# 71 groups instead of 74 take SIGN, 16 products left out, and new orders on all five engines

## Chip, core and metric

The kernel runs on one core of one Trainium2 chip. The metric is the device time of one execution in microseconds (us). A core has five engines with a queue each: PE (TensorE, matmul; PEld is its weight load), DVE (VectorE), ACT (ScalarE), POOL (GpSimd) and SP (SyncE, which here only issues DMAs). Each runs its own list of instructions strictly in the order in which they were written and waits on semaphores for the others.

## What is computed

Attention that keeps, for each query, the 32 largest scores, then a two-layer net with squared ReLU on the joined heads. Cut to what matters:

```python
# q, k, v: (8, 8, 576, 64)
scores = q @ k.T / sqrt(64)
kth = 32nd largest of each row
attn = softmax(where(scores >= kth, scores, -1e9))
x = (attn @ v) as (4608, 512)
h = x @ w_in            # 512 x 2048
out = (max(h, 0) ** 2) @ w_out
```

## The kernel before

**Groups.** The queries are cut into 144 groups, each 128 queries of two heads (the last 64 queries of two pairs of heads share a group). For each group, in this order: PE multiplies q and k (`mm`, L875) into a PSUM area of three banks; ACT copies the 2 x 576 scores out (L1053); DVE folds them with three maxima of PSUM and SBUF (L1131); POOL makes the matching minima with two integer operations (L1126); DVE finds the 8 largest of several candidate lists (MAX8, L1178, L1173), strikes them out (MATCH_REPLACE8, preceded by a MATCH_VALUE_LOAD, both L1193) and ends with the 32nd largest (`kth`, L1196); ACT makes a mask from it (L1219, two instructions); PE transposes the scores and adds the mask (L878, L875); ACT takes the exponential (L1285); PE multiplies with v. A second PSUM area of the same kind holds the transposed scores.

**SIGN groups.** Of the three strikings of a group (`c8`, `c16`, `c24`), the last can be done in another way: for the groups in `VOID`, DVE issues no MATCH_REPLACE8 for `c24`; ACT computes SIGN of the difference to the 24th value, with an accumulated sum (L1183: two ACTIVATEs, each with a read of the accumulator), and POOL multiplies (L1186). `VOIDS` holds the ranges of these groups, and the sums go to `signs`.

**The net.** Every 256 or 128 finished rows are transposed by DMA into `xt`, PE multiplies with `win`, ACT applies ReLU (L1443), POOL or ACT squares (L1458, L1461), PE multiplies with `wo`, ACT copies out (L1479), and SP stores. The last rows go another way (`feed_last`: ReLU at L1527, squares on DVE at L1530).

**The verdict.** The fast way to find the 32nd value can fail on rare inputs. `verdict` gathers checks on DVE (L1703 to L1729), PE sums them (L1731), and DVE writes `flag` (L1733). Each engine loads `flag` at the end (L1778), and branches to a full second computation if it isn't 0. So nothing ends before `flag`. Three checks per range in `VOIDS` are tensor operations (L1703): `x` compares the 23rd and 24th values, `y` subtracts from `signs`, `z` compares the 22nd and 24th values.

**What sets the order.** The program first makes a list of operations, then `arrange` puts them on the engines by the table `ORDER`: one row of operation numbers per engine. A negative number in PE's row is an idle product (three 128x128 products with `ident_bf`, which leave nothing behind); the operations of `fill` are products of `ones_bf` with itself, 512 columns, whose result isn't used either. `SLOT` gives each PSUM tile its area. The waits follow from the order.

Of the kernel before, what the change touches and what calls it, by code (L numbers as in the profile page):

```python
# [32 lines left out]
        "90 91 92 93 94 95 96 97 98 2541 2542 2543 2547 2574 2579 101 100 104 106 102 2613 2614 2615 2620 2648 -4979 -4979 -4979 -4979 -4979 126 119 129 134 "  # L33
        "2686 136 2688 135 2687 -5025 2577 2693 148 149 2756 153 159 2758 2757 2605 2721 167 169 2607 2646 183 2763 188 3230 190 -4991 195 -4991 -4991 3232 "
        "3231 2675 2792 204 210 207 209 2677 2719 2874 -5037 219 -5037 -5037 222 -5037 -5037 226 -5037 -5037 240 -5037 -5037 2904 2748 244 241 -5049 2933 2750 "
        "-5149 2790 245 3298 2963 2819 256 257 274 3299 2992 3300 275 276 278 2900 3026 2821 2931 283 293 292 3369 3057 2959 294 3371 -5408 3370 -5408 -5408 "
        "-5169 3085 2961 2902 2990 2826 2827 2829 2830 3116 3018 2833 3437 2834 -5195 -5195 -5195 3144 3438 -5249 3053 3236 3020 -5215 3439 -5215 3083 2836 "
        "2837 3055 3264 2840 2841 3112 3304 -5244 -5244 -5244 2847 2848 2843 2844 3142 2850 3332 3114 2851 3171 2854 2857 3375 3173 2856 2861 2860 2864 2855 "
        "2866 3262 3403 2859 2858 2865 3291 2869 3942 2870 3443 3330 2871 3293 2868 2867 3471 3179 3180 3182 3183 3359 3186 3187 3189 3190 3553 3401 3193 3194 "
        "3361 3584 3196 3197 3943 3430 3200 3201 3613 3944 3432 3469 3203 4010 3204 3643 -5459 4011 4012 -5459 3672 3207 3498 3210 4081 3208 3214 -5471 3706 "  # L40
        "3500 3212 3580 3209 3211 3213 4082 3611 3737 4083 3582 -5535 3765 3217 4149 3222 3639 3218 3223 3224 3220 3221 3219 3670 3796 3505 3506 3508 3509 "
        "3824 3512 3513 3515 3516 3641 3698 3519 3520 3522 3523 3948 3733 3526 4150 3527 3976 4151 3529 3530 3700 3763 4016 3533 3538 3735 3534 3792 3539 4044 "
        "3822 3535 3536 3540 3537 3794 3851 4087 3543 3544 3853 3548 4115 3549 3546 3974 4622 3547 3550 3545 4003 4624 4623 4155 4042 4005 3859 3860 4183 3862 "
        "3863 3866 3867 4071 3869 3870 4265 4113 3873 3874 4073 -5809 4295 3876 4142 3877 3880 3881 4324 4144 4690 3907 3909 3910 3908 4181 4692 4691 4355 "
        "3918 3919 3912 3914 3913 3915 4210 3920 3921 3923 3924 3925 3926 4384 3883 4212 3884 4418 4761 4762 4291 3887 4763 3892 3889 3891 3893 3894 4449 3890 "
        "3888 4293 4322 3897 3902 3900 3899 3904 4351 4477 4829 4382 3903 4353 3898 3901 4508 3929 3932 4830 3931 3930 4410 3933 4536 4412 3934 3935 3936 4831 "
        "4445 4628 4217 4218 4447 4475 4220 4221 4656 4504 4224 4225 4227 4228 4696 4506 4534 4231 4232 4234 4235 4724 4238 4239 4241 4242 4245 4248 4247 4246 "
        "4563 4767 4251 4252 4565 4795 4255 4250 4262 4249 4261 4256 4257 5334 4260 4654 4258 4259 4835 4683 4571 4572 4574 4575 4722 4863 4578 -6143 -6143 "
        "4945 4579 4581 4582 4751 4685 4585 4586 4975 4588 4589 4793 4592 4593 4595 4596 5004 4822 4753 5335 5336 5402 5034 4824 5403 5404 4861 5063 5473 4890 "
        "4599 5474 4606 4600 5098 4892 4971 4603 4604 5475 4601 4605 4602 4973 5129 5002 4609 4612 4611 4616 5157 5541 4610 5030 4615 4897 4898 5188 4613 4614 "  # L50
        "5032 5061 4900 4901 4904 4905 5216 4907 4908 5090 4911 4912 4914 5340 5125 5092 4915 -6361 5368 5127 5155 5542 4918 4919 -6377 5543 5408 4921 4922 "
        "4925 4928 5184 4929 5436 5214 4927 4930 5186 4931 4926 5243 5479 4932 5245 5366 4935 4937 4936 4938 5507 4940 4939 4942 6014 4941 5395 5547 6015 5397 "
        "5434 5251 5252 5254 5255 5575 5258 5259 5261 5262 5657 5265 5266 5268 5269 5463 5272 5299 5273 5300 5301 5302 5687 5304 5310 5305 5307 5306 5313 5312 "
        "5311 5505 5315 5317 5318 5465 5316 5716 5534 6023 5275 5276 5746 5536 6016 5573 5279 6024 5281 5284 5282 5280 6025 5283 5775 5602 5289 5285 5295 5286 "
        "5292 5809 5604 5290 5296 5291 5293 6062 5294 5840 6063 6064 5683 5321 5326 5325 5685 5714 5869 5323 5328 6071 5742 5327 6072 5900 5773 5322 5324 5744 "
        "6073 -6920 -6920 5928 5801 5609 5610 5612 5613 6029 5803 5836 5616 5617 5619 5620 6077 5867 5623 5624 5838 -6771 -6771 6144 5626 5627 5630 5631 5633 "
# [607 lines left out]
def bass_top_k_attn__then__act_relu_squared_kernel(  # L664
# [91 lines left out]
    VOIDS = (3, 137, 2), (6, 137, 20)  # L756
# [1087 lines left out]
```

## Time and profile before

| | |
|---|---|
| median of 3 runs | 744.73 us (744.64 to 747.37) |
| the profiled execution | 746.16 us, of which the span of its instructions is 744.3 us and 1.9 us lie around it |
| busy | PE 706.4, DVE 719.4, ACT 717.3, POOL 685.9 us |

The span runs from the first to the last instruction. An engine's busy time is the union of its instructions' records. Records of DVE and ACT overlap, since the next one starts before the one ahead has ended; what an instruction costs its engine is read from start to start. A short wait can lie hidden below such an overlap.

### The profile page before, as it was taken

How to read it: one execution, taken by the hardware profiler on the slowest of the kernel's cores; microseconds unless marked ns; L12 is line 12 of the kernel's file. 1: busy time of each engine (PE TensorE's matmuls, PEld its weight loads, DVE VectorE, ACT ScalarE, POOL GpSimd, SP SyncE). 2: the span in 40 equal slices, each digit the busy share in tenths (PEclk: the TensorE clock that was granted, in tenths of full speed). 3: DMA queues.
4: the chain of work that ended last, by engine and by line, in shares of the span. 5: the costliest groups of instructions: out<-in, count | busy, mean ns of one | idle time of the engine just before them, and what ended most of it. 6: DMA issues, size and time to landing. Idle time of an engine off the chain costs nothing.

```text
span 744.3 us, 27788 instructions
## 1 busy us (share of the span) xinstructions
PE 706.4 (95%) x10712; PEld 530.0 (71%) x10712; DVE 719.4 (97%) x3397; ACT 717.3 (96%) x1276; POOL 685.9 (92%) x529
## 2 busy tenths in 40 slices
PE   8898899999999999989999999999999999999997
PEld 4565777767677676767778677777777777777876
DVE  5999999999999999999999999999999999999996
ACT  4899999999999999999999999999999999999984
POOL 3799999999999999999999999999999999999971
PEclk9999999999999999999999999999999999999999
DMA  9766544254342432134311733121643115211101
GB/s 181 165 170 175 134 102 73 70 87 78 67 84 48 84 79 52 44 70 85 82 35 36 125 92 64 27 48 56 117 75 80 28 44 93 58 35 32 37 16 51
DMA packets 172730, 57.31 MB, mean 77 GB/s; under 512 B 157744, under 2 KB 164912, under 8 KB 172592
## 3 DMA queue, kind: packets, MB, share of 16 engines
q1 hardware_dynamic: 164528, 51.19, 30.2%
q0 software_dynamic: 7392, 4.13, 4.7%
q8 instruction: 85, 1.39, 0.8%
q14 instruction: 53, 0.43, 0.2%
q10 hardware_dynamic: 672, 0.16, 0.1%
HBM read 40.83 MB, written 13.57 MB: 73 GB/s over the span
## 4 chain that ended last, share of the span: by engine, by line
ACT 59%; PE 21%; DVE 16%; issue 3%; ACTq 0%
PE ps L875 17%; ACT w L1219 16%; ACT p L1285 12%; ACT s L1053 12%; ACT g L1443 6%; ACT s L1183 5%; DVE s L1131 4%; PE ps L878 4%; DVE s L1193 3%; DVE c L1178 3%; ACT av L1388 2%; DVE kth L1196 2%; DVE s L1173 2%; ACT o L1479 2%; ACT g L1461 1%
## 5 line engine op out<-in xcount | busy, mean ns | idle before, releaser
L1126 POOL TENSOR_TENSOR u<-s 128x864 int32<-128x864 int32 x142 | 244.7, 1723 | 22.1 <-DVE s L1131 20.8
L1219 ACT ACTIVATE w<-s,kth 128x576 bf16<-128x576 f32 x286 | 245.9, 918 | 2.9 <-DVE kth L1196 2.8
L1126 POOL TENSOR_TENSOR s<-s,u 128x864 int32<-128x864 int32 x142 | 243.1, 1714 | 3.2
L1178 DVE MAX8 c<-s 128x8 f32<-128x106 f32 (+2 forms) x864 | 203.3, 264 | 0.0
L1131 DVE TENSOR_TENSOR s<-ps,s 128x288 f32<-128x288 f32 x432 | 192.2, 445 | 9.9 <-ACT s L1053 7.7
L875 PE MATMUL ps<-qk 64*128 64x192 f32 (+3 forms) x1280 | 179.5, 430 | 8.5 <-DVE s L1131 4.6
L1053 ACT COPY s<-ps 128x1152 f32<-128x1152 f32 (+1 forms) x145 | 180.2, 1244 | 4.8 <-PE ps L875 4.1
L1285 ACT ACTIVATE p<-ps 128x1152 bf16<-128x1152 f32 x143 | 180.9, 1265 | 1.7 <-PE ps L875 1.5
L1193 DVE MATCH_REPLACE8 s<-c,s 128x92 f32<-128x92 f32 (+2 forms) x716 | 179.5, 254 | 0.0
L875 PEld LDWEIGHTS ps<-qk 64*128 64x128 f32 (+1 forms) x1280 | 130.8, 176 | 39.3 <-DVE s L1131 11.4
L875 PE MATMUL ps<-wo,g 128*128 128x512 bf16 (+1 forms) x592 | 144.5, 374 | 0.8 <-ACT qk L1007 0.4
L875 PE MATMUL ps<-xt,win 128*128 128x256 bf16 (+1 forms) x1280 | 130.7, 252 | 1.7 <-ACT g L1443 0.9
L1196 DVE MAX8 kth<-s 128x8 f32<-128x296 f32 x288 | 127.9, 454 | 0.3 <-POOL s L1186 0.2
L1173 DVE MAX8 s<-s 128x8 f32<-128x288 f32 x288 | 125.3, 446 | 0.3 <-POOL s L1126 0.2
L878 PEld LDWEIGHTS ps<-ident,s 64*128 64x128 f32 x2592 | 97.0, 139 | 35.9 <-ACT w L1219 13.5
L878 PE MATMUL ps<-ident,s 64*128 64x64 f32 x2592 | 112.4, 228 | 8.8 <-ACT w L1219 7.1
L875 PEld LDWEIGHTS ps<-xt,win 128*128 128x128 bf16 x1280 | 99.0, 98 | 21.0 <-issue 4.0
L1443 ACT ACTIVATE g<-ps 128x512 bf16<-128x512 f32 x140 | 98.2, 745 | 0.2
L1458 POOL TENSOR_TENSOR g<-g 128x1024 bf16<-128x1024 bf16 x50 | 94.6, 1892 | 3.8 <-ACT g L1443 3.7
L875 PEld LDWEIGHTS ps<-wo,g 128*128 128x128 bf16 x592 | 50.2, 98 | 48.1 <-issue 4.3
L1183 ACT ACTIVATE s<-s,c 128x140 f32<-128x140 f32 x148 | 76.4, 558 | 0.0
L875 PEld LDWEIGHTS ps<-vb,p 128*128 128x128 bf16 (+1 forms) x1600 | 54.6, 101 | 22.7 <-ACT p L1285 4.5
(92 smaller groups left out, 779.0 us busy)
## 6 DMA issues: line engine op xcount, KB each, us to landing
out_dram<-o SPq DMA_DIRECT2D x32, 256.0 KB, 2.8
rk<-in_k_dram SPq DMA_DIRECT2D x63, 128.0 KB, 2.6
rq<-in_q_dram SPq DMA_DIRECT2D x62, 128.0 KB, 2.6
s<-s SPq DMA_DIRECT2D x144, 32.0 KB, 1.9
g<-in_moe_w_in_dram SPq DMA_DIRECT2D x8, 512.0 KB, 4.4
g<-in_moe_w_out_dram SPq DMA_DIRECT2D x8, 512.0 KB, 4.1
vd<-in_v_dram POOLq DMA_DIRECT2D x14, 288.0 KB, 4.5
vb<-vd SPq DMA_DIRECT2D x56, 64.0 KB, 2.3
```

Source lines behind the costliest of these rows:

```text
L875: return pe.matmul(o, l, r, start=start, stop=stop, skip_group_check=True)
L878: return pe.matmul(o, i, ident, is_transpose=True, skip_group_check=True, **kw)
L1053: return pl.op("act", .14 + 2 * (c1 - c0) / 1200, pl.at("copy", tg - LEAD + 1), lambda: act.copy(at(st)[:, :, c0:c1], two(banks(ss)[:, FIR ...
L1126: return pl.op("gp", dur, prio, lambda: gp.tensor_tensor(o().bitcast(I32), x().bitcast(I32), y().bitcast(I32), op), **kw)
L1131: return dve(.36, lambda: vec.tensor_tensor(o(), two(banks(ss)[:, FIRST_AT + c:], SECOND, QUART), x(), ALU.max), r=[ss], **kw)
L1173: prev[i] = [dve(.0685 + HALF / 960, lambda i=i: vec.max(area(LIST, LIST + 8, i), area(LESS, LESS + HALF, i)), after=prev[i] + [low], hold ...
L1178: lambda i=i, t=t, span_=span_: vec.max(eighth(t, i), span_(i)),
L1193: lambda i=i, t=t, span_=span_: vec.match_replace(span_(i), eighth(t, i), span_(i), NEG), hold=[st])]
L1196: ks.append(chain(kth, i, prev[i], .0685 + (8 + HALF) / 960, lambda i=i: vec.max(eighth(kth, i), area(BIGS - QUART, LIST + 8, i)), hold=[st]))
L1219: masks[i:] = [pl.op("act", .77, pl.at("mask", tw + .8 * i), lambda i=i: act.activation(at(wt)[:, i, :], at(st)[:, i, 0:S], ACTF.Relu, bia ...
L1285: return act.activation(at(pt)[:, :, :].rearrange("p c (h q) -> p h c q", h=2), bass.AP(x.tensor, x.offset, [x.ap[0], [APART, 2], [64, 9], ...
L1443: return act.activation(at(g)[:, g0:g0 + 512], bank(hh)[:, 0:512], ACTF.Relu)
```

## The change

- The second range of `VOIDS` has a step of 40 instead of 20: groups 26, 66 and 106 no longer take SIGN, which leaves 71 of 74. The checks on this range work on 4 groups instead of 7.
- Of PE's row, 5 of 56 `fill` products and 11 of 46 idle products are left out.
- All five rows of `ORDER` and all of `SLOT` are new. The table is one line shorter, so every line below it has a number lower by one (L1131 is L1130).

```diff
 ORDER = {
     "pe": (
...
-        "8240 8244 8246 8284"),
...
+        "8216 8231 8228 8234 8238 8236 8235 8237 8239 8242 8243 8240 8241 8281"),
...
@@ -753,7 +752,7 @@
     rzall = sb("rzall", [P, NALL])
-    VOIDS = (3, 137, 2), (6, 137, 20)
+    VOIDS = (3, 137, 2), (6, 137, 40)
     VLAST = max(v for _, v, _ in VOIDS)
```

PE's queue from its start, before and in the change (`rq` and `rk` are the first loaded pieces of q and k, `qk` their transposes; the `ones_bf` products are `fill`):

```order
L875 MATMUL ps<-ones_bf 128x512 x9
L878 MATMUL ps<-ident,rq 128x128
L878 MATMUL ps<-ident,rk 128x128 x4
L878 MATMUL ps<-ident,rk 128x64
L875 MATMUL ps<-qk 128x192
```

```order
L874 MATMUL ps<-ones_bf 128x512 x7
L877 MATMUL ps<-ident,rq 128x128
L877 MATMUL ps<-ident,rk 128x128 x4
L877 MATMUL ps<-ident,rk 128x64
L874 MATMUL ps<-qk 128x192
```

Two of the nine products ahead of the first transposes stand further back. The five `fill` products that are left out are late ones, at groups 116 to 142, and the 11 idle ones come from the middle of the row.

ACT's queue some 15 instructions after its start, before and in the change (`s` are the scores of a group, `w` its mask, `p` its exponentials, `win` a weight that is cast, `qk` the next pair's transposes):

```order
L1053 COPY s<-ps 128x2x576 x2
L1665 CAST win<-g 128x1024
L1006 COPY qk<-ps 128x512
L1008 COPY qk<-ps 128x2x64
L1219 ACTIVATE w<-s,kth 128x576 x2
L1007 COPY qk<-ps 128x512
L1285 ACTIVATE p<-ps 128x2x9x64
L1053 COPY s<-ps 128x2x576
```

```order
L1052 COPY s<-ps 128x2x576 x2
L1005 COPY qk<-ps 128x512
L1006 COPY qk<-ps 128x512
L1218 ACTIVATE w<-s,kth 128x576
L1007 COPY qk<-ps 128x2x64
L1664 CAST win<-g 128x1024
L1218 ACTIVATE w<-s,kth 128x576
L1052 COPY s<-ps 128x2x576
L1664 CAST win<-g 128x1024
L1284 ACTIVATE p<-ps 128x2x9x64
```

The copy of group 4's scores stood behind the first exponential and now stands ahead of it, and the cast of the first weight moved behind the copies of `qk` and the first mask.

DVE's queue around `x` of the verdict: before, it stood some 40 rows ahead of the last `kth`:

```order
L1196 MAX kth<-s 128x8
L1193 MATCH_REPLACE s<-c,s 128x92
L1178 MAX c<-s 128x8
L1703 TENSOR_TENSOR c<-c 128x2x67
L1193 MATCH_REPLACE s<-c,s 128x106
```

In the change it stands right behind the last `kth` of the last group (before, `y` stood there):

```order
L1177 MAX c<-s 128x8
L1192 MATCH_REPLACE s<-c,s 128x2x70
L1195 MAX kth<-s 128x8
L1702 TENSOR_TENSOR c<-c 128x2x67
L1211 TENSOR_SCALAR w<-s,kth 128x512
L1394 RECIPROCAL rzall<-av 128x4
```

And `y` has moved behind operations that wait for PE, ahead of the first L1530 (now L1529):

```order
L1374 COPY xt<-ps 128x128
L1712 TENSOR_REDUCE fone<-kth 128x1
L1724 TENSOR_REDUCE fone<-rzall 128x1
L1702 TENSOR_TENSOR signs<-signs,c 128x2x67
L1724 TENSOR_REDUCE fone<-rzall 128x1
L1529 TENSOR_TENSOR g<-g 128x256
```

Behind the last of the five L1530 stood 15 instructions of DVE up to the sum on PE; in the change 23 of them follow it, the small checks of the second range among them.

## Rows read from the trace of the kernel before

**Rows 1.** Busy time of each engine in four of five stretches of the span, in us: the stretch and its length, then PE, PEld, DVE, ACT and POOL, each with its number of instructions, the granted TensorE clock (1.00 is full speed), the share of DMA and GB/s.

```profile
0.00:20.00 20.00, 16.50 (x93) 9.31 (x93) 11.26 (x45) 9.57 (x15) 6.93 (x38) 1.00 0.90 178
20.00:80.00 60.00, 51.90 (x767) 37.74 (x769) 58.55 (x279) 55.98 (x95) 54.81 (x45) 0.94 0.68 163
80.00:700.00 620.00, 598.33 (x9196) 451.49 (x9194) 612.77 (x2909) 619.80 (x1115) 600.33 (x431) 1.00 0.33 68
...
720.00:744.30 24.30, 20.16 (x320) 16.28 (x318) 17.26 (x76) 14.33 (x28) 5.43 (x5) 0.98 0.12 39
```

**Rows 2.** Who waited for whom: of DVE in 80 to 700 us, and then of ACT and of DVE in 20 to 80 us (total, times, longest, in us).

```profile
DVE s L1131 <- ACT s L1053: 4.1, 18, 0.4
...
ACT p L1285 <- PE ps L875: 1.5, 2, 1.0
ACT s L1053 <- PE ps L875: 1.2, 2, 1.0
ACT w L1219 <- DVE kth L1196: 1.0, 1, 1.0
...
DVE s L1131 <- ACT s L1053: 1.3, 2, 0.8
```

**Rows 3.** ACT in order of time at one SIGN group: start, length, instruction. The two instructions left out repeat the first two.

```profile
34.02 0.44 ACT L1183 ACTIVATE s<-s,c 128x140 f32<-128x140 f32 x1
34.33 0.23 ACT L1183 ACTIVATION_READ_ACCUMULATOR s<-s,c 128x1 f32 x1
...
34.81 0.40 ACT L1388 COPY av<-ps 128x260 f32<-128x260 f32 x1
```

**Rows 4.** DVE in order of time at one striking of `c24` (the 140 columns), up to the start of the next instruction; and the group of POOL's multiplications on the page.

```profile
23.95 0.07 DVE L1193 MATCH_VALUE_LOAD s<-c,s 128x8 f32 x1
24.01 0.29 DVE L1193 MATCH_REPLACE8 s<-c,s 128x140 f32<-128x140 f32 x1
24.21 0.29 DVE L1178 MAX8 c<-s 128x8 f32<-128x140 f32 x1
...
L1186 POOL TENSOR_TENSOR s<-s 128x280 f32<-128x280 f32 x74 | 50.5, 683 | 10.2 <-ACT s L1183 9.6
```

**Rows 5.** The two large L1703 and their neighbours on DVE, the second stretch of the same list, and POOL's squares at those times.

```profile
712.59 1.69 DVE L1703 TENSOR_TENSOR c<-c 128x134 f32<-128x134 f32 x1
714.19 0.08 DVE L1193 MATCH_VALUE_LOAD s<-c,s 128x8 f32 x1
...
725.75 0.47 DVE L1196 MAX8 kth<-s 128x8 f32<-128x296 f32 x1
726.14 1.39 DVE L1703 TENSOR_TENSOR signs<-signs,c 128x134 f32<-128x134 f32 x1
727.45 0.47 DVE L1212 TENSOR_SCALAR w<-s,kth 128x512 bf16<-128x512 f32 x1
...
728.74 0.49 DVE L1703 TENSOR_TENSOR c<-c 128x14 f32<-128x14 f32 x2
...
712.11 1.90 POOL L1458 TENSOR_TENSOR g<-g 128x1024 bf16<-128x1024 bf16 x1
...
725.38 1.89 POOL L1458 TENSOR_TENSOR g<-g 128x1024 bf16<-128x1024 bf16 x1 [2.76 <-ACT g L1443]
```

**Rows 6.** The end on DVE, in order of time from the last square, and the chain that ended last where it passes the first L1703.

```profile
737.62 0.43 DVE L1530 TENSOR_TENSOR g<-g 128x512 bf16<-128x512 bf16 x1 [0.65 <-ACT g L1527]
...
738.33 0.37 DVE L1718 TENSOR_TENSOR c<-s,kth 128x42 f32<-128x42 f32 x2
...
740.57 0.16 DVE L1729 TENSOR_SCALAR fone<-fone 128x2 f32<-128x2 f32 x1
741.02 0.16 DVE L1733 TENSOR_REDUCE flag<-ps 1x1 int32<-1x12 f32 x1 [0.29 <-PE ps L1731]
...
712.67 1.60 DVE c L1703
```

**Rows 7.** The first products of PE in order of time; ACT's two loads of `rk`; and the loads' time from issue to landing (the last number).

```profile
1.07 4.02 PE L875 MATMUL ps<-ones_bf 128*128 128x512 bf16 x9 [1.07 <-DVE ones_bf L1622]
5.15 0.47 PE L878 MATMUL ps<-ident,rq 128*128 128x128 f32 x1
7.25 1.24 PE L875 MATMUL ps<-qk 64*128 64x192 f32 x8 [0.67 <-DVE qk L934]
...
0.76 1.25 ACTq L904 DMA_DIRECT2D rk<-in_k_dram  x2
...
rk<-in_k_dram ACTq DMA_DIRECT2D x1, 32.0 KB, 3.5
```

**Rows 8.** Busy time by stretch again, around the two stretches in which the granted clock fell; and PE's score product in the first of them.

```profile
24.00:26.00 2.00, 2.00 (x14) 1.59 (x8) 2.00 (x13) 1.13 (x1) 2.00 (x2) 0.50 1.03 292
26.00:28.00 2.00, 1.88 (x10) 0.67 (x8) 1.19 (x5) 1.75 (x3) 1.80 (x3) 0.85 0.70 61
66.00:68.00 2.00, 0.80 (x10) 0.73 (x14) 2.00 (x12) 2.00 (x4) 2.00 (x3) 0.89 0.67 151
68.00:70.00 2.00, 2.00 (x28) 1.26 (x23) 2.00 (x12) 1.76 (x2) 2.00 (x2) 0.50 0.52 85
70.00:72.00 2.00, 2.00 (x45) 1.53 (x42) 2.00 (x10) 1.39 (x5) 2.00 (x2) 0.75 0.80 277
...
23.93 2.27 PE L875 MATMUL ps<-qk 64*128 64x192 f32 x8
```

More of the change, by code (lines that the diff above doesn't have):

```diff
@@ L32 @@
     "pe": (
[43 rows of a table removed]
[L76 removed]
[38 rows of a table removed]
[L115 removed]
[121 rows of a table removed]
[42 rows of a table added]
+    "act": (
[38 rows of a table added]
+    "dve": (
[121 rows of a table added]
 }
 SLOT = (
[L239 to L240 removed]
+    "01010101010101010000100101000001010000000000001000000000100001110000000000010000000000100000000010000000000000000001000000100000000100001000"
+    "00000000000001000000000000000000100000000000000000000000000001100000001000000000010000000000000000000000000000000000000000000000000000000000"
     "00000000000000000000000000000000000000000000000000000000000000000000000000000000000000000000000000000000000000000000000000000000000000000000"
@@ L267 @@
-    "110016121001100010100111110001200111110011010030100100400010010512000006010100000101110000000011110100001201010010130012020001213011")
+    "00000000000000000000000000000000000000000000000000000000000000000000000000000000000010001000101011001100010101102000213000010011102002040101"
+    "15001000001130131610001001011010111102113000111100121002000013111111400000511110000160012110011101100011021112030000101000110211300000104040"
+    "00400000511010000010111602120000000000050100111111120000110010210031112140000100010110211311011051110101600010000101010112121200000030011011"
@@ new lines @@
+    "41100050001006021210101000001011021131100104015000002030101000012110100113140113020204100000100410100501111600001011011001001101100010000101"
+    "10201301001020110011300000411011150002161000100000010010111201120010113111214001000100110021131101100102101501000610111011513100002120110001"
+    "00002041002010113001001113101104010205000000000110120030100116110100100000011111012001213111010114000111151010060101000001201011000001011021"
+    "13010010401510000011101200110300100011402101411120500000000010300060101001010011150401010000020011101011100211300011131010101401110502101161"
@@ new lines @@
+    "00200011000101100100102010103000011401120500000010011012103010010021010110110116111010003121011413100000111004100100111210020001001310000401"
+    "01100050000160101110002001100011100111102103000111210120300000014000015101110016011200000011110000120101000010110201301001001040011210101300"
+    "00000001111115121004010100005101011160111110100000001111110010011110120010111301101000400110005011001001110101610100100000110101010000021001"
+    "00001011000301000104001001015111010160011101211001000303111140410100000100010001112011111001010010020000211100003001000004110010150011100001"
@@ L270 @@
+    "110016121011000010100011100000200011110111010130110100400110010512100016011100000101010100000010110101000201110010030002020101203011")
 class Pool:
```

13 lines of the change are left out of this document (removed), and 397 rows, old and new, of the table ORDER.

## Prediction, made before the change was run

> **What bounds the kernel now.** I read the busy time by stretch first, because a share over the whole span mixes the ramps with the steady part. From 80 to 700 us ACT is busy for 619.80 of 620 us, DVE for 612.77, POOL for 600.33 and PE for 598.33 [rows 1]. ACT shows no idle time to speak of and DVE 7.2 us, so the steady part has two engines at their limit, ACT a little ahead. Then the waits: of DVE's idle time there, 4.1 us in 18 waits are its first fold waiting for ACT's copy of the scores [rows 2], so DVE, where it stands still, stands still for ACT. PE and POOL wait for both and set nothing over this stretch. The ramps differ: from 20 to 80 us ACT is idle for 4.0 us and DVE for 1.5, and in the last 24 us DVE and ACT are idle for 7 and 10 [rows 1]. In order, the views say: take work off ACT first, off DVE next, and in the last 40 us off DVE alone, for there the chain that ended last runs through DVE, with one L1703 of 1.60 us in it [rows 6].
>
> **SIGN on three groups fewer.** On ACT a SIGN group takes the queue from 34.02 to 34.81, 0.79 us from the start of its first instruction to the start of the next kind [rows 3]; three groups are 2.4 us. DVE gets back two strikings per group; from the value load at 23.95 to the next instruction at 24.21 one costs 0.26 us [rows 4], six 1.6 us. POOL loses three multiplications of 0.68 us [rows 4], 2.0 us that it has idle anyway. In the steady part ACT's queue becomes 2.4 us shorter and DVE's 1.6 longer. If the end there moves up by 2.4, DVE is left with 7.2 - 1.6 - 2.4 = 3.2 us of idle time: it fits, if DVE has work ready. I take **-2.4**. Bounds: 0 if DVE's stalls all stay, -2.4 at most from this alone.
>
> **The check `x` moves behind the last `kth`.** Ahead of the last `kth` DVE loses 1.60 us of work (712.59 to 714.19 [rows 5]), which cancels the 1.6 us of strikings, so DVE has the same work up to its last `kth` as before. What `x` costs at its new place needs care. Of three L1703 of this size, one took 1.69 us, one 1.39, and the third, with a small one, 0.49 for both [rows 5]. The two long ones ran while POOL squared (712.11 to 714.01, and 725.38 to 727.27) and ended 0.27 and 0.26 us after it; the third began after that. So most of the long ones is waiting for POOL, not work. In the change `x` takes the place at which `y` stood, and POOL's last squares stand where they did; there it should be held as `y` was, 1.3 us. `y` goes ahead of the first L1530, where POOL has nothing left, and should take 0.4. I put the exchange behind `kth` at 0; the bounds are +0.3 (1.6 instead of 1.3) and, if the two miss each other, -0.9.
>
> The Trainium skill states a rule for this (SBUF — State Buffer, "Who interferes with whom"): a VectorE instruction with two SBUF inputs and a GpSimd instruction that reads SBUF need the same port pair, and the later one waits until the other has ended. The rows agree, with 0.27 and 0.26 us from POOL's end to DVE's. By the durations alone, `y` would push the first L1530 back by 1.4; by the rule it doesn't.
>
> **Two products fewer ahead of the first transposes.** The nine start at 1.07 and take 4.02 us, 0.45 each; the first transpose starts at 5.15 [rows 7]. Seven would end 0.9 us earlier, at about 4.2. The last piece of `rk` is ACT's second load: issued by about 1.3, in the middle of ACT's 0.76 to 2.01, with 3.5 us to landing, so there at about 4.8 [rows 7]. The transposes then wait for it and not for the products: 5.15 - 4.85, **-0.3**. The bounds are 0 and -0.9.
>
> **The new order from 20 to 80 us.** ACT waited 1.5 and 1.2 us for PE and 1.0 us for a `kth`, DVE 1.3 us for copies, 0.81 of it between 26 and 28 [rows 2, 8]. Those are the stretches where the fifth full copy stood behind the first exponential; in the change it stands ahead, and a 1-us cast no longer stands ahead of the first mask. DVE is the fuller engine here (1.5 us idle of 60 [rows 1]), so no more than 1.5 can be gained. I take half, **-0.8**.
>
> **The new order in the steady part.** The change moves nearly every row, and no row of the trace prices that. The bound is what is left of DVE's idle time, 3.2 us, on the side of gain; on the side of loss, nothing excludes waits as long as those of today once more (4.1). Of the 4.1 us of waits, all of one kind and each 0.4 or less [rows 2], I take half as avoidable by setting copies earlier: **-2.0**. ACT's records overlap (the first of [rows 3] ends at 34.46, the next starts at 34.33), so ACT too has waits that its busy time hides; otherwise this gain couldn't exist on it.
>
> **The 16 products.** The five late ones and the 11 idle ones stand in stretches in which PE waits for ACT or DVE; they cost at most 0.45 each on PE, which has 22 us idle in the steady part [rows 1, 7]. I cost them at 0; what hides them is PE's waiting, and what they may have kept up is the clock (below).
>
> **The end.** `flag` can't come before DVE's last checks. Between the last L1530 and the sum stand 15 instructions, and from the start of that L1530, 737.62, to the end of the last of them, 740.73 (740.57 plus 0.16), it is 3.1 us; the flag ends at 741.18, 3.6 us after 737.62 [rows 6]. In the change eight more follow. The small ones among them are like L1718, where two took 0.37 and so start 0.14 apart [rows 6]; reductions over 134 columns are somewhat longer. Eight times 0.1 is +0.8. Part of it may be swallowed if the last L1530 comes earlier: **+0.5**, bounds 0 and +0.8. What is late next is the load of `flag` on every engine, and nothing hides that.
>
> **The sum:** -2.4 - 0.3 - 0.8 - 2.0 + 0.5 = -5.0. On the profiled execution's own time of 746.16 that is 741.2. That execution lay 1.4 above the median of the three runs, 744.73, so I predict 739.7 for the median. A measurement of this kernel tells about 0.5%, 3.7 us, from no change: faster begins at 741.0.
>
> **The rivals.**
>
> *DVE becomes the bound and the order gains nothing (0.27).* For it: DVE gets 1.6 us more in a stretch where it is 98.8% busy, and its idle time is cut up into pieces of 0.4 us or less [rows 1, 2]. Against it: what it waits for there is ACT, which is relieved. Then only part of ACT's 2.4 arrives: -1.2 - 0.3 + 0 + 0 + 0.5 = -1.0, so 743.7, within 742 to 746.
>
> *The waits for copies vanish altogether (0.10).* Then all 3.2 us of idle time in the steady part go, the full 1.5 of the ramp, and waits hidden under ACT's and DVE's overlaps as well, which I bound by as much again as the visible 4.1: -2.4 - 0.3 - 1.5 - 3.2 - 2.0 = -9.4, 735.3, or some us below.
>
> *The first score runs at half clock (0.12).* The first products of 512 columns took 0.45 us each, so PE began at its lower level, 1.2 GHz; the first score, at 7.25, took 1.24 us, and one at a granted clock of 0.50 took 2.27 [rows 7, 8]. With seven products and a pause ahead of the transposes the clock may rise later, and the first score costs 1.0 more. The Trainium skill (TensorE: Matmul & The Clock Gate, "What's actually happening") says that PE starts at half rate and that its own work releases it, which speaks against fewer products ahead; the trace agrees that it starts there. With everything else as forecast: -5.0 + 0.3 + 1.0 = -3.7, 741.0.
>
> *The clock falls in the steady part (0.06), the one that ends slower.* After 66 to 68 us, in which PE worked 0.80 of 2 us, its clock fell to 0.50, and ACT stood idle for 0.24 and 0.61 us in the next 4 [rows 8]: 0.85 per fall. The five products left out late in the program and the 11 idle ones stood in such pauses. Six more falls take the 5.0 back; at eleven, +9.4, the kernel is slower by over 0.5% (749). Against it: from 80 to 700 the clock is 1.00 with PE 96% busy [rows 1], and the products left out are few there.
>
> **How the numbers follow.** The forecast has 0.45, with its own range of 737 to 742. Faster by over 0.5% is nearly all of the forecast (0.41), half of the half-clock case (0.06) and all of the vanished waits (0.10): 0.57. Slower is the falling clock, 0.06. Within 0.5% is the rest, 0.37. The range from 734 to 745.5 leaves out the falling clock, the lower part of the vanished waits and the upper part of the first rival, about 0.2.
>
> **What would show it.** Right: DVE's first fold waits for copies for under 2.5 us from 80 to 700; ACT still without idle time there, with the stretch shorter; the first transpose at about 4.85; a long L1703 right behind the last `kth` and a short one after 732. Wrong: ACT with several us of idle time in the steady part (then DVE bounds, and SIGN groups were taken from the wrong engine); the first score at over 2 us; granted clock below 1.00 between 80 and 700; the time from last L1530 to `flag` above 4.2 us, where it was 3.6.

## Result, and the profile after

The changed kernel takes 749.87 us (median of 6 runs, 749.34 to 751.62), the kernel before 744.93 beside it: a ratio of 1.0065 [1.0046, 1.0083]. It is slower, where 739.7 was forecast. Five single executions of 1090 to 2238 us, two of the kernel before and one each of three kernels below, are left out of every ratio, and nothing here shows what lengthened them. Its profiled execution took 750.28 us, with a span of 748.5, 4.2 more than before; the sum had -5.0, so 9.2 us have to be found.

Busy time by stretch in the changed kernel (columns as in [rows 1]):

```profile
0.00:20.00 20.00, 12.41 (x51) 6.61 (x53) 9.61 (x37) 5.83 (x10) 7.18 (x40) 0.88 0.96 190
20.00:80.00 60.00, 51.34 (x769) 37.50 (x766) 57.60 (x275) 57.16 (x96) 53.46 (x44) 0.98 0.64 162
80.00:700.00 620.00, 589.18 (x9047) 446.74 (x9111) 609.90 (x2906) 616.69 (x1097) 596.00 (x423) 1.00 0.33 68
...
720.00:748.50 28.50, 23.63 (x380) 18.83 (x378) 20.91 (x98) 17.17 (x32) 9.09 (x8) 1.00 0.10 35
```

Who waits from 80 to 700 us, first DVE, then ACT (total, times, longest):

```profile
DVE s L1192 <- POOL u L1125: 3.0, 6, 0.9
DVE s L1130 <- ACT s L1052: 2.7, 12, 0.4
DVE kth L1195 <- POOL s L1185: 1.7, 4, 1.0
DVE s L1172 <- POOL s L1125: 0.6, 1, 0.6
...
ACT w L1218 <- DVE kth L1195: 1.8, 4, 1.2
ACT w L1218 <- DMA s<-s: 1.3, 1, 1.3
```

ACT, busy throughout before, now has 3.3 us of idle time here. DVE waits less for ACT's copies (2.7 us, before 4.1 [rows 2]), but 5.3 us for POOL, which the view of before shows with 0.4 us in two waits. POOL has three multiplications less than before and is late all the same.

To place the loss I took ACT's copies of the scores, one per group, as mile posts: the 12th and the last of the 144, before,

```profile
59.66 1.15 ACT L1053 COPY s<-ps 128x1152 f32<-128x1152 f32 x1
...
711.33 1.26 ACT L1053 COPY s<-ps 128x1152 f32<-128x1152 f32 x1
```

and in the change:

```profile
62.58 1.15 ACT L1052 COPY s<-ps 128x1152 f32<-128x1152 f32 x1
...
716.37 1.24 ACT L1052 COPY s<-ps 128x1152 f32<-128x1152 f32 x1
```

The head is 2.9 us longer (forecast -1.1), the stretch between the two 2.1 longer (5.04 - 2.92; forecast -4.4), and the end 0.8 shorter (4.2 - 5.0; forecast +0.5). The two misses of 4.0 and 6.5 are the 9.2 and 1.3 more, which the end gives back. The head of the kernel before varies too: in five profiles with its order and at most one early cast this copy lies between 58.2 and 59.8.

**The head.** What moved first stands on an engine that I didn't look at. POOL issues 14 DMAs that cast v (`vd<-in_v_dram`, 288 KB each); before, they start at 5.8, 25.4 us and so on to 628. In the change three start within 8 us:

```profile
3.70 0.88 POOL L1671 DMA_DIRECT2D vd<-in_v_dram  x1
5.28 0.62 POOL L1671 DMA_DIRECT2D vd<-in_v_dram  x1
7.63 0.62 POOL L1671 DMA_DIRECT2D vd<-in_v_dram  x1
```

DMA in the first 12 us, in the change (queue: packets, MB, share of the 16 engines; issues: size, median us to landing):

```profile
q0 software_dynamic: 1279, 0.72, 47.8%
...
vd<-in_v_dram POOLq DMA_DIRECT2D x3, 288.0 KB, 6.7
...
rk<-in_k_dram SPq DMA_DIRECT2D x3, 128.0 KB, 5.8
```

and before:

```profile
q0 software_dynamic: 528, 0.29, 18.4%
...
rk<-in_k_dram SPq DMA_DIRECT2D x3, 128.0 KB, 4.1
```

The next pair's three loads of `rk`, issued at 7.9, 8.5 and 9.1 us, share the engines with the casts. They land after 6.05, 5.76 and 6.49 us, where the kernel before, with one cast beside them, has 4.19, 4.11 and 4.06 (the x3 of the views counts two of them and the first pair's). The chain of work through the head of the change shows what that costs:

```profile
9.08 6.49 DMA rk<-in_k_dram
...
15.70 1.50 PE ps L877 x6
...
18.04 2.85 PE ps L874 x7
...
20.91 1.13 ACT s L1052
...
22.06 0.46 DVE s L1130
```

The load takes 6.49 us. PE, busy for 0.9 of the 4 us before, has a granted clock of 0.50 from 16 to 22 us (half level, 1.2 GHz), and DVE's fold waits 4.4 us for a copy.

**The steady part.** One stall on SP's queue, in order of time:

```profile
125.93 1.28 SPq L1411 DMA_TRANSPOSE xt<-x  x1
127.25 3.53 SPq L1417 DMA_TRANSPOSE xz<-x  x2
130.83 1.24 SPq L1198 DMA_DIRECT2D s<-s  x2
```

and ACT's mask behind it:

```profile
130.36 1.13 ACT L1052 COPY s<-ps 128x1152 f32<-128x1152 f32 x1
132.78 0.78 ACT L1218 ACTIVATE w<-s,kth 128x576 bf16<-128x576 f32 x1 [1.29 <-DMA s<-s]
```

The move `s<-s`, which the mask needs, stands behind three transposes that hold SP's queue for 4.9 us. And one stall on POOL, the longest of three places (194, 412 and 482 us) where a minimum that DVE waits for stands a few rows behind a cast:

```profile
479.14 1.26 POOL L1396 TENSOR_TENSOR x<-av,rzall 128x640 bf16<-128x640 f32 x1 [0.97 <-DMA xt<-x]
480.36 1.71 POOL L1125 TENSOR_TENSOR s<-s,u 128x864 int32<-128x864 int32 x1
482.01 0.68 POOL L1671 DMA_DIRECT2D vd<-in_v_dram  x1
```

POOL waits 0.97 us for a transpose (issued at 474.28, landed 4.75 later, median 2.5 in this kernel), then spends 0.73 on issuing a cast and its marker (482.01 to 482.74). DVE's value load at 485.21 waits 0.92 for POOL's next minimum, and ACT stands for a mask up to 486.46. At the other two places DVE waits 0.59 and 0.71, without the transpose.

### The profile page after: what moved, and what is told of

The parts are those of the page before. It is cut to its first block, busy times and chain, and to the rows that moved or that the text cites. A ratio compares the mean times of both kernels' runs of the same rounds, so it can differ in the third digit from the quotient of the medians.

```text
span 748.5 us, 27668 instructions
## 1 busy us (share of the span) xinstructions
PE 696.2 (93%) x10604; PEld 526.4 (70%) x10674; DVE 717.9 (96%) x3409; ACT 716.7 (96%) x1264; POOL 685.0 (92%) x526
## 4 chain that ended last, share of the span: by engine, by line
ACT 48%; PE 17%; DVE 15%; POOL 11%; issue 4%; DMA 2%; SPq 1%; POOLq 0%; ACTq 0%; DVEq 0%
PE ps L874 14%; ACT w L1218 13%; ACT s L1052 10%; ACT p L1284 9%; ACT g L1442 5%; ACT s L1182 4%; DVE s L1130 4%; POOL u L1125 4%; POOL s L1125 4%; DVE s L1192 3%; PE ps L877 3%; DVE c L1177 3%; DVE kth L1195 2%; DVE s L1172 2%; POOL g L1457 2%
## 5 line engine op out<-in xcount | busy, mean ns | idle before, releaser
L1218 ACT ACTIVATE w<-s,kth 128x576 bf16<-128x576 f32 x286 | 236.1, 863 | 3.2 <-DVE kth L1195 1.8
L1177 DVE MAX8 c<-s 128x8 f32<-128x92 f32 (+2 forms) x864 | 203.6, 264 | 0.1
L1130 DVE TENSOR_TENSOR s<-ps,s 128x288 f32<-128x288 f32 x432 | 191.8, 445 | 10.8 <-ACT s L1052 9.0
L874 PE MATMUL ps<-qk 64*128 64x384 f32 (+3 forms) x1280 | 179.3, 428 | 8.6 <-ACT p L1284 4.5
L1192 DVE MATCH_REPLACE8 s<-c,s 128x106 f32<-128x106 f32 (+2 forms) x722 | 181.5, 255 | 0.0
L1052 ACT COPY s<-ps 128x1152 f32<-128x1152 f32 (+1 forms) x145 | 173.0, 1194 | 5.8 <-PE ps L874 5.0
L1284 ACT ACTIVATE p<-ps 128x1152 bf16<-128x1152 f32 x143 | 173.1, 1214 | 0.7 <-PE ps L874 0.5
L874 PE MATMUL ps<-wo,g 128*128 128x512 bf16 (+1 forms) x522 | 130.2, 373 | 10.0 <-issue 7.2
L877 PEld LDWEIGHTS ps<-ident,s 64*128 64x128 f32 x2592 | 95.2, 139 | 37.8 <-ACT w L1218 14.1
L1442 ACT ACTIVATE g<-ps 128x512 bf16<-128x512 f32 x140 | 91.2, 682 | 0.2 <-PE ps L874 0.2
L1182 ACT ACTIVATE s<-s,c 128x140 f32<-128x140 f32 x142 | 68.1, 503 | 0.0
```

What stands on the lines that cost most here:

```text
L874: return pe.matmul(o, l, r, start=start, stop=stop, skip_group_check=True)
L877: return pe.matmul(o, i, ident, is_transpose=True, skip_group_check=True, **kw)
L1052: return pl.op("act", .14 + 2 * (c1 - c0) / 1200, pl.at("copy", tg - LEAD + 1), lambda: act.copy(at(st)[:, :, c0:c1], two(banks(ss)[:, FIR ...
L1130: return dve(.36, lambda: vec.tensor_tensor(o(), two(banks(ss)[:, FIRST_AT + c:], SECOND, QUART), x(), ALU.max), r=[ss], **kw)
L1177: lambda i=i, t=t, span_=span_: vec.max(eighth(t, i), span_(i)),
L1192: lambda i=i, t=t, span_=span_: vec.match_replace(span_(i), eighth(t, i), span_(i), NEG), hold=[st])]
```

## Experiments

Two pairs of theories. For the head: the three early casts, or the weight load among the first loads. For the steady part: ACT paces it and POOL's and SP's places disturb it, or DVE has become the bound (my first rival). Each ratio is to the kernel before on the same chip. Edits are shown as rows of the engine named.

**The early casts moved (change, POOL).** Two of the three go behind the minima of groups 23 and 32 (126 and 174 us):

```diff
 L1625 CAST ident_bf<-ident 128x128
-L1671 DMA vd<-in_v_dram 512x288
 L1633 MEMSET heads 64x1
...
 L1640 MEMSET vb 128x8
-L1671 DMA vd<-in_v_dram 512x288
 L1125 TENSOR_TENSOR u<-s 128x864
```

> The changed kernel, but the two value casts that POOL issues early beside the first (3.7 and 7.6 us) stand behind POOL's minima of groups 23 and 32, where the kernel before has its third and fourth. Theory A (the three casts of 288 KB take the DMA engines from the loads of q and k in the first 16 us): the second rk lands some 4 us earlier, DVE's wait of 4.5 us ahead of its fold at 21.9 falls to under 1 us, the time falls by 3.5 to 4.5, from 749.9 to 745.4 to 746.4. Rival B (the weight load that SP issues ahead of rq is what delays them): no change, above 749. Rival C (the fewer products and the new order on ACT in the head): no change, above 749.

750.5 us, 1.006 [1.0036, 1.0083]: no gain. Yet the wait at 17.6 fell from 4.4 to 0.4 us and copy 12 came 1.1 us before that of the old kernel, as the casts' theory wants. The lead over the change reached 4.1, and 3.0 of it was lost at one place, where ACT then stood for a mask (the chain of work has a move `s<-s` there, not DVE):

```profile
127.65 3.91 DMA s<-s
...
131.64 0.78 ACT L1218 ACTIVATE w<-s,kth 128x576 bf16<-128x576 f32 x1 [3.55 <-DVE s L1192]
```

One cast now fell among SP's transposes at 126 us, and the move behind them took 3.91 us (1.87 in the change). The casts do delay the head; where a cast goes matters as much as where it leaves.

**The weight load moved instead (change, SP).**

```diff
 L955 DMA rk<-in_k_dram 64x2x64
-L1661 DMA g<-in_moe_w_in_dram 128x1024
 L954 DMA rq<-in_q_dram 128x4x64 x2
...
 L1198 DMA s<-s 128x64
+L1661 DMA g<-in_moe_w_in_dram 128x1024
```

> The changed kernel, but SP's first weight load (512 KB, at 11.7 us) stands behind the next loads of rq and rk and the first group's s<-s, as in the kernel before; the casts stay early. Theory A (casts): the late rk was issued at 9.1 us, before the weight load, so at most the next pieces gain: 749 to 750, under 0.7 us less. Rival B (weight load): 2 us or more less, 748 or under.

749.64, 1.0044 [1.003, 1.0059]: about the change itself, and `rk` still takes 6.73. The weight load alone isn't it.

**The same three casts early in the kernel before (POOL).**

```diff
 L1631 TENSOR_SCALAR plus_bf<-ident 128x128
+L1672 DMA vd<-in_v_dram 512x288
 L1634 MEMSET heads 64x1
...
-L1640 MEMSET vb 128x2x64 x3
+L1640 MEMSET vb 128x2x64
+L1672 DMA vd<-in_v_dram 512x288
+L1640 MEMSET vb 128x2x64 x2
```

> The kernel before, with nothing changed but that POOL issues three value casts in the first 8 us (as the changed kernel does) instead of one. Theory A: 3.5 to 4.5 us more than 744.9, so 748.4 to 749.4, and DVE waits for the copy of the third group's scores at about 18 to 22 us. Rivals B and C: 744.5 to 745.5.

746.39, 1.0006 [0.999, 1.0022]: not slower by the ratio. The load isn't quite that of the change: the third cast started at 12.3 us, behind POOL's wait for `av`, and not at 7.6, and the three `rk` took 5.0 us in the median, between the 4.1 of the kernel before and the 6.05 of the change. In the profile the third copy came 2.5 us late; the waits that the old order has at 20 to 26 us took up a part of it, and 1.4 stayed. So early casts delay `rk` in either order. That the new order pays more because it has no slack behind them fits this, but isn't shown apart from the later third cast.

**SIGN alone (kernel before, new `VOIDS`, old order).** DVE strikes `c24` of groups 26, 66 and 106.

```diff
-    VOIDS = (3, 137, 2), (6, 137, 20)
+    VOIDS = (3, 137, 2), (6, 137, 40)
```

> The kernel before in its own order, with SIGN taken from groups 26, 66 and 106 alone (their ACT and POOL instructions left out, two strikings each put into DVE's row five places behind their c24). Theory D (ACT bounds the steady part, as forecast): 1.2 to 2.4 us less, 742.5 to 743.7. Rival E (DVE bounds, ACT's 100% busy share hides slack): no change or up to 1.6 more, 744.9 to 746.5.

746.72, 1.0013 [0.9998, 1.0028]: the 2.4 us of ACT didn't arrive; between the two mile posts this profile is 2.0 us longer than that of the kernel before. Behind group 26 PE had little to do, and the granted clock fell (stretches as in [rows 1]):

```profile
148.00:150.00 2.00, 0.52 (x3) 0.11 (x2) 2.00 (x8) 2.00 (x4) 1.14 (x2) 1.00 0.58 131
...
152.00:154.00 2.00, 2.00 (x9) 1.19 (x8) 2.00 (x9) 2.00 (x4) 2.00 (x3) 0.50 0.50 110
```

ACT waited 1.2 us for PE there; at another group DVE's strikings made the next SIGN wait for `c24`. Here work taken off ACT didn't become time, because what feeds ACT didn't come earlier. I chose the places of the strikings in DVE's row; whether others would do better wasn't run.

**More work on ACT, more on DVE (kernel before).** The extra results are used by nothing; nothing of the computation is left out.

```diff
-lambda: act.copy(at(avs)[:, u0:u0 + nu, :], ...)
+lambda: [act.copy(y, ...) for y, k in [(more[:, :, :], 2)] * (gi % 2) + [(at(avs)[:, u0:u0 + nu, :], nu)]][-1]
```

```diff
-vec.max(area(LIST, LIST + 8, i), area(LESS, LESS + HALF, i))
+[vec.max(x, area(LESS, LESS + HALF, i)) for x in [more[:, n - n % 8:n - n % 8 + 8]] * (n % 8 == 4 and i == 0) + [area(LIST, LIST + 8, i)]][-1]
```

> The kernel before with an extra ACT copy of 130 columns ahead of every second copy of av (L1388), some 45 in all, 0.14 to 0.25 us each: 6 to 11 us of work more for ACT, nothing else. Forecast's theory D (ACT paces the steady part): the whole of it shows, 6 us or more. Theory E (ACT's busy share of 100% hides waits under overlapping records, DVE paces): less than half of what is added shows.

> The kernel before with one more MAX8 over 288 columns on DVE in every eighth group, 18 in all at 0.36 us, 6.5 us of work more for DVE, nothing else (the result of the extra ones is not used). Theory D (ACT paces, DVE has 7 us to spare): 0 to 3 us. Theory E (DVE paces): 5 us or more.

63 copies more on ACT, 0.15 us each from start to start, 9.6 in all, gave 754.67, 1.0125 [1.0103, 1.0146], that is +9.3. 18 MAX8 more on DVE, 0.36 each, 6.5 in all, gave 745.69, 1.0003 [0.9989, 1.0017]. The steady part with more on DVE, and DVE's waits in it:

```profile
80.00:700.00 620.00, 597.12 (x9167) 450.93 (x9167) 615.59 (x2923) 619.57 (x1113) 599.25 (x429) 1.00 0.32 68
```

```profile
DVE s L1131 <- ACT s L1053: 2.3, 10, 0.4
```

DVE absorbs nearly all of the 6.5 us (the interval allows a loss of up to 1.3) although it was busy for 612.77 of 620 [rows 1], and ACT stays full. 5.4 of them lie in this stretch, where its busy time grew by 2.8 only, so a part of that busy time was waiting. So ACT paces the kernel before. The change puts 1.6 us more on DVE and was to shorten the stretch by 2.4, together less than 6.5; that my first rival falls for the new order as well is inferred from this, not run there.

**SP's move ahead of the transposes (first experiment's kernel, SP).**

```diff
 L965 DMA vb<-vd 64x64 x2
+L1198 DMA s<-s 128x64 x2
 L1411 DMA_TRANSPOSE xt<-x 128x4x128
 L1417 DMA_TRANSPOSE xz<-x 128x1x64 x2
-L1198 DMA s<-s 128x64 x2
```

> The changed kernel with the two early value casts moved back (as in a_casts_late) and, in SP's row, the two small moves of scores (L1198, groups 22 and 24) ahead of the three transposes that SP issues at 125.9 to 130.8 us, instead of behind them. Theory F (a_casts_late gained 3.9 us up to 120 us and gave 3.6 of them back at 127 to 135, because ACT's mask of group 22 waits for a move that stands in SP's queue behind transposes of 1.25 to 3 us of issue each; what SP does there isn't earlier when ACT is): the gain stays, ACT's copies from group 30 on lie 0 to 1 us behind those of the kernel before, 745.0 to 747.0. Rival G (something else, as POOL or the transposed values, gives it back at that place): 749 or more, as a_casts_late.

748.68, 1.0048 [1.0023, 1.0073]. The mask no longer waits, but the next on ACT's queue does:

```profile
127.44 0.77 ACT L1218 ACTIVATE w<-s,kth 128x576 bf16<-128x576 f32 x1
132.64 1.08 ACT L1442 ACTIVATE g<-ps 128x512 bf16<-128x512 f32 x2 [4.43 <-PE ps L874]
```

The ReLU waits for products of `xt`, whose transpose goes 1.05 us later than in the first experiment and runs beside the cast of 125.46. Here the stall moved to the next user of the same transfers.

**Four edits at once.** Beside that swap and the late weight load, the two casts go to about 71 and 91 us, and POOL's `x` at 479 goes three later:

```diff
-L1396 TENSOR_TENSOR x<-av,rzall 128x640
 L1125 TENSOR_TENSOR s<-s,u 128x2x432
...
 L1125 TENSOR_TENSOR u<-s 128x864
+L1396 TENSOR_TENSOR x<-av,rzall 128x640
```

> The changed kernel with four rows moved: the two early casts (to POOL's place behind groups 12 and 16), the moves of groups 22 and 24 ahead of the transposes, SP's first weight load as in the kernel before, and POOL's L1396 that waits 0.97 us for a transfer at 479 behind the next three operations. Theory F, and H (the stalls of 0.7 to 1.5 us after 120 are single places where POOL or SP is late, and each can be taken away by itself): 743.5 to 746.0. Rival E in its strict form (DVE bounds, and with 1.6 us more work on it the new order can't be faster than the kernel before): 746 or more.

751.41, 1.0074 [1.0053, 1.0096]. It led the change by 3.2 us up to 481 and lost about 4 at 486. SP's transpose waits for `x`, and PE for the transpose, with the products of `xt` ahead of the next pair's transposes in its queue:

```profile
483.75 1.89 PE L874 MATMUL ps<-xt,win 128*128 128x256 bf16 x8 [3.27 <-DMA xt<-x]
```

The granted clock is 0.50 from 484 to 488 us, behind that wait, and the same eight products take 1.05 in the change. The edit of `x` was wrong and is dropped.

**The head alone.** Casts at 33 and 84 us, the weight load late, the move first; `x` left in place:

```diff
 L1664 CAST win<-g 128x1024
+L1671 DMA vd<-in_v_dram 512x288
 L1185 TENSOR_TENSOR s<-s 128x2x2x70
```

> The changed kernel with the two early casts moved to places where POOL stood idle for 0.45 and 0.30 us anyway (37.4 and 88 us, clear of the transposes at 124 to 131), SP's first weight load as in the kernel before, and the moves of groups 22 and 24 ahead of the transposes. Theory F (the loss has single places; a_four kept 3.0 us of its gain up to 481 us with nearly this and lost 4 us only where my fourth edit held up a load): 745.5 to 747.5, and ACT's copies from group 30 to 96 lie 3 us or more earlier than in the changed kernel. Rival I (interlock: whatever is gained at one place is lost at the next input that isn't there yet, as in b_71): 749 or more.

746.58, 1.0024 [1.0003, 1.0044]; in the profile 4.9 us below the change. **Five later casts moved too**, each to a place where POOL's next minimum isn't awaited, and `xt` ahead of `xz` at 472:

```diff
+L1671 DMA vd<-in_v_dram 512x288
 L1125 TENSOR_TENSOR u<-s 128x864
 L1457 TENSOR_TENSOR g<-g 128x1024
 L1185 TENSOR_TENSOR s<-s 128x2x2x70
 L1125 TENSOR_TENSOR s<-s,u 128x2x432
-L1671 DMA vd<-in_v_dram 512x288
```

> As a_head, and five later casts moved from behind or ahead of full stretches of POOL (189, 407, 409, 473, 482 us) to places where POOL stood idle for 0.3 to 0.6 us, and at 472 us the transfer that POOL waited for at 479 issued ahead of the two beside it. Theory F with ACT as the pace (b_act_more): DVE's waits for POOL between 80 and 700 us, 5.3 us in 11, fall to under 2.5, and the stall of 3.2 us at 482 to 487 goes: 741.5 to 744.0, faster than the kernel before. Rival I: as a_head, 745 to 748.

747.24, 1.0029 [1.0012, 1.0046]. The stalls at 193, 411 and 481 us gave back 0.4, 0.5 and 1.5, as expected; this execution's head was 3.2 longer though its `rk` landed as fast (2.7 us in the median, before this edit 3.0), and 2.0 were lost at 134, where ACT's ReLU again waited for products of `xt`. The gain at the three places is seen in the trace, not in the median.

What made this head longer is no load and no row that the edit moved, but PE's first score, here and then in the change:

```profile
7.00 2.29 PE L874 MATMUL ps<-qk 64*128 64x192 f32 x8 [0.58 <-DVE qk L933]
...
6.55 1.24 PE L874 MATMUL ps<-qk 64*128 64x192 f32 x8 [0.67 <-DVE qk L933]
```

The products ahead of it start at the same times in both (the first transpose at 4.75). The second and third copies then come 2.9 and 3.2 us later than in the profile before this edit. Three of the eleven profiles with the change's first products show it (also the late weight load, and the last kernel below), none of the six with the old ones; why one execution has it and another doesn't isn't shown.

**Transposes ahead of the value loads, the last early cast to 22 us, and DVE's checks into waits.** SP (first) and DVE, where 17 of the last checks go ahead of the last squares:

```diff
+L1411 DMA_TRANSPOSE xt<-x 128x4x128
 L961 DMA vb<-vd 128x4x64 x2
 L965 DMA vb<-vd 64x64 x2
-L1411 DMA_TRANSPOSE xt<-x 128x4x128
```

```diff
+L1702 TENSOR_TENSOR c<-c 128x2x67
+L1702 TENSOR_TENSOR signs<-signs,c 128x2x67
 L1369 RECIPROCAL rzall<-ps 128x2
...
+L1716 TENSOR_TENSOR c<-kth,c 128x2x144
 L1529 TENSOR_TENSOR g<-g 128x256 x2
```

> a_all with three more edits: the transfer of xt that PE waits 1.65 us for at 125 to 127 issued ahead of the value loads beside it on SP; the one value cast that was left in the first 8 us moved to 27 us; and on DVE 17 of the last checks moved into the two waits of 2.7 and 1.0 us ahead of the last squares. Theory F (single places, each to be taken away by itself, ACT paces the rest): 741.0 to 744.0, faster than the kernel before. Rival I (what is gained is lost at the next input): 745 to 747.

745.0, 1.0004 [0.9988, 1.0021]. One stall was left, and the chain of work names it:

```profile
434.76 0.68 POOL vd L1671
...
435.94 6.74 DMA xt<-x
...
442.82 1.05 PE ps L874 x8
```

A cast issued 1.2 us ahead of the transposes; `xt` took 6.74 us instead of the usual 2.5, and PE stood until then. **The first cast of the kernel before to 22 us**, as control:

```diff
-L1672 DMA vd<-in_v_dram 512x288
 L941 CAST vb<-av 128x10x64
...
 L1126 TENSOR_TENSOR u<-s 128x864
+L1672 DMA vd<-in_v_dram 512x288
```

> The kernel before with its first value cast (288 KB, issued at 5.8 us) moved to about 27 us, nothing else. Theory A in its lesser form (a cast under way while the first pieces of q and k are loaded delays them, by an amount that differs from run to run): 0.5 to 1.5 us less than the kernel before, and a narrower spread. If a single cast does no harm: 744.5 to 745.7, spread as before.

745.15, 1.0005 [0.9995, 1.0015]: `rk` lands after 2.5 us instead of 4.1, and the time is the same, so one cast in the head is hidden there.

**That one cast moved from 434.8 to about 410 us.**

```diff
+L1671 DMA vd<-in_v_dram 512x288
 L1125 TENSOR_TENSOR u<-s 128x864
...
 L1396 TENSOR_TENSOR x<-av,rzall 128x512
-L1671 DMA vd<-in_v_dram 512x288
```

> a_best with one cast alone moved: the one that fell at 434.8 us, 1.2 us ahead of a transposing transfer of xt that then took 6.7 us to land (2.6 is the median), goes to about 410, with no such transfer within 10 us. Theory J (a value cast under way stretches the transposes, PE waits for xt, ACT for PE): PE's wait of 1.9 and ACT's of 1.5 at 442 to 444 go, 1.3 to 1.8 less in the same executions: 743.0 to 744.0 and faster than the kernel before. Rival I: the wait only moves, 744.5 to 746.

741.8 (741.54 to 743.38), 0.9959 [0.9943, 0.9975]: faster than both kernels. Its steady part and DVE's waits there; ACT has none in that view:

```profile
80.00:700.00 620.00, 601.88 (x9178) 450.24 (x9176) 614.05 (x2930) 619.71 (x1104) 599.97 (x429) 1.00 0.32 68
```

```profile
DVE s L1130 <- ACT s L1052: 2.5, 11, 0.4
DVE s L1192 <- POOL u L1125: 0.9, 3, 0.3
DVE kth L1195 <- POOL s L1185: 0.2, 1, 0.2
```

**The two halves apart.** First the change with only the casts' places of the last kernel, then with only its other edits (SP's four, DVE's end); their rows are those above.

> The changed kernel with only its value casts moved, to the places that they have in a_best2; SP's and DVE's rows are those of the change. If the casts are the main cause: 5 to 6 us less than the changed kernel's 749.9 (3.9 in the head, 2.3 where POOL was late), 744 to 745; the mask that waits for a move behind the transposes at about 127 still waits, 1.4 us or more. If casts and SP's order only help together: 747 or more.

> The complement: the changed kernel with a_best2's four edits in SP's row and its order of the last checks on DVE, the casts where the change has them. If the casts are the main cause: 1.5 to 3 us less than the changed kernel, 747 to 748.5. If SP's order is the main cause: 745 or less.

Casts alone: 745.32, 0.9998 [0.9984, 1.0012]. With no cast in the first 12 us, the three `rk` take 2.7 us in the median, DVE's wait of 4.4 at 17.6 is gone, and the clock from 16 to 22 is 1.00. The rest alone: 746.88, 1.0014 [1.0003, 1.0025]; there `rk` still takes 6.79 and the clock from 16 to 22 is 0.72. From the change's 1.0065 that is -5.0 and -3.8 us; both together gave -7.9. In the profiled spans it is -5.7 and -3.0, and -8.8 for both. So they add up nearly, and moving casts alone takes the change back to the time of the kernel before. DVE's checks are 1.2 of the second half, the rest is SP's. That the casts are the larger half rests on the profiles, since the two intervals overlap. But for the one cast above, these edits weren't made in the kernel before, so how much of them mends the change and how much would help the old order too is open.

## Why the prediction was wrong, step by step

- **What bounds the kernel** was right for ACT: +9.6 on it gave +9.3. That DVE is at its limit next was not: 98.8% busy, it still took 6.5 us more for 0.2, at most 1.3. The share of busy time didn't show its slack.
- **SIGN, -2.4.** The price from the rows was taken as time saved, with 0 as bound. Alone, in the old order, it gave nothing. In the mended kernel the stretch between the two mile posts is 2.0 shorter than before, which would fit SIGN with nothing from the order; no run shows that it is SIGN's.
- **The new order in the steady part, -2.0, is the step that failed most,** with SIGN's on which it sits: +2.1 instead of -4.4. I priced DVE's waits for copies, which did fall from 4.1 to 2.7, and named "waits as long as those of today once more" as the bound for loss without asking whose. The order listed PE, ACT and DVE for me; POOL's rows and SP's, where the new waits come from, stood unread, though POOL's work and SP's transfers release both. In the traces of the two halves, moving casts gives back 0.4, 0.5 and 1.5 us at the three places on POOL, and SP's order 1.4 at 126 to 133. That is nearly all of the 4.1 by which the mended kernel's stretch is shorter than the change's; the other 2.4 of the forecast never came, and why is open. The wait for copies, 2.7, also missed the 2.5 that I had named as the sign of being right.
- **The ramp, -0.8, failed too:** with the first products' -0.3 the head was to be 1.1 shorter and is 2.9 longer. The first fold came at 8.26 instead of 8.96, but by 22 us the gain was gone in `rk`'s 6.49 us. The sum looked at no load behind the first and had no term for the two casts that moved into the head; with them moved out the twelfth copy came 1.1 earlier than in the kernel before.
- **The first products, -0.3.** The first transpose came at 4.75 us (forecast 4.85), but not for my reason. The last piece of `rk` had landed at 4.24, and PE went to the transposes straight from the products, which took longer than 0.45 each:

```profile
1.07 3.89 PE L874 MATMUL ps<-ones_bf 128*128 128x512 bf16 x7 [1.07 <-DVE ones_bf L1621]
```

 So the number is luck.
- **`x` behind `kth`, 0.** Right. `x` at its new place, `z` and `y`, on DVE in the change:

```profile
730.20 1.21 DVE L1702 TENSOR_TENSOR c<-c 128x134 f32<-128x134 f32 x1
734.94 0.38 DVE L1702 TENSOR_TENSOR c<-c 128x134 f32<-128x134 f32 x1
...
736.83 0.38 DVE L1702 TENSOR_TENSOR signs<-signs,c 128x134 f32<-128x134 f32 x1
```

 POOL's last square runs from 729.25 for 1.89, to 731.14; the long one ends 0.27 later, at 731.41, as those in [rows 5] did. The rule quoted from the Trainium skill (SBUF — State Buffer, "Who interferes with whom") agrees with this row too.
- **The end, +0.5.** From the last square to `flag`:

```profile
740.71 0.91 DVE L1529 TENSOR_TENSOR g<-g 128x512 bf16<-128x512 bf16 x2 [0.54 <-ACT g L1526]
...
745.42 0.16 DVE L1732 TENSOR_REDUCE flag<-ps 1x1 int32<-1x12 f32 x1 [0.29 <-PE ps L1730]
```

 The second of the pair starts at 741.20; the flag ends at 745.58, 4.4 later: the +0.8 that was the bound, and above the 4.2 that I had named as a sign of being wrong. The end as a whole, from the last copy on, is 0.8 shorter, so the work ahead of the last square gained 1.6. With 17 checks moved into waits it is 2.1 shorter than before.
- **The 16 products, 0.** In the change's profile the first score runs at 1.24 us, and the granted clock is 1.00 in every 2 us from 80 to 700. So neither clock rival made this execution slow, and the falling clock, the only rival that ended slower, falls. The half-clock rival doesn't fall: its sign, a first score of over 2 us, came in three other profiles of these first products (2.29). It costs the score 1.05, as the rival had it, but the head 3.2 with one early cast; with three, where the head waits for `rk` anyway, it is hidden (in the last kernel above the second copy is 2.9 later than in the change, the twelfth 0.3 earlier). No run puts the products back by themselves, so their price of 0 stands untested.
- **The rivals.** "Slower" came by a mechanism that was on no list. ACT's idle time in the steady part, 3.3 us, was named as a sign that DVE bounds; here it came by way of POOL's and SP's places. The sum of the vanished waits leaves out the end's +0.5 and takes 2.0 for hidden waits that its text bounds at 4.1, which changes no outcome.

That the mended kernel's profiled 741.54 lies beside the sum's 741.2 is chance: its parts are -0.5, -2.0 and -2.1, not -1.1, -4.4 and +0.5.

What stays open: what decides whether the first score takes 1.24 or 2.29 us, and how often it does in executions that weren't profiled; and which part of the 2.0 us that the mended kernel gains in the steady part is SIGN's.

## What to carry to other kernels

When a change reorders everything, read the queues of the engines that only issue transfers as closely as those that compute: list every DMA that moved, and price what shares the engines with it and what stands behind it. Here the engine at 100% set the pace, and one at 98.8% took 6.5 us more nearly free; an extra copy of an instruction that an engine already runs tells which it is. Where orders are as tight as here a mended stall uncovers the next one, so edits are judged in the trace, place by place, and kept or dropped there; that took the change from 0.65% slower than the kernel before to 0.4% faster.

## What the runs showed of the hardware

- A cast of 288 KB in flight stretches what runs beside it: the next pair's three `rk` took 2.4 to 2.7 us in the median of a profile without a cast beside them, 2.7 to 4.3 with one, 5.0 to 6.1 with three; one `xt` took 6.74, usually 2.5. The casts themselves took 3.8 to 6.1 us before and up to 7.4 in the change. The Trainium skill (DMA: Bandwidth & Descriptors, "Anatomy of one DMA — SWDGE (gpsimd) path") has 2.0 us plus the bytes over 436 GB/s, an estimate of 2.7 us for 288 KB; the traces disagree with it at every cast. The same page of the Trainium skill ("Queues, rings and completion order") says that a DMA engine takes turns between its queues packet by packet, which fits transfers that stretch each other.
- A transpose holds SP's queue for 1.1 to 2.3 us at its issue (1.23 in the median of the change's 70), and what stands behind it on SP waits for that, whatever it needs itself.
- PE's first score took 1.24 us in fourteen profiles and 2.29 in three. In the change and in the kernel with the five later casts the first transpose starts at 4.75 alike, and the column of the granted clock reads 1.00 from 6 to 10 us in both, though one has 1.24 and the other 2.29: there the pace is seen in the durations alone.
